# A shared first relu, a moved copy and a swapped sum at the start of a gated-attention kernel

The change halves the first score group's relu between ScalarE and VectorE, lets VectorE rather than ScalarE copy the first turned block of z, and forms the sum of the second output half of the first slot before that of the first.

## Chip, cores and metric

The kernel runs on one core of one Trainium2 chip. The metric is the device time of one execution in microseconds (us). The first three runs of the kernel before gave a median of 1193.32 us (1192.68 to 1193.82). The span of a trace is about 1.8 us shorter than the time of the same run. Kernels are compared only within the same rounds.

## The reference, cut to what matters

```python
# B, S, D = 8, 3008, 256; d_qk = 64; d_ff = 2048
scores = (1.0 / S) * z @ z.transpose(0, 2, 1)
attn = np.maximum(scores, 0.0) ** 2
x = (u * (attn @ v)).reshape(B * S, D)
h = x @ w_in
out = ((h * np.cos(h)) @ w_out).astype(np.float32)      # 24064 x 256
```

The scores are symmetric, so the kernel computes a block (J, I) once and gets (I, J) by transposing it.

## The kernel before

Work goes in slots, one for each batch and 512 rows. Each score group is two matmuls into a two-bank accumulator pair E (512 columns each); ScalarE takes the relu into r (fp16); VectorE squares r into a piece A; and value matmuls multiply A by v into the accumulators M[0], M[1] or into a pair E. `gate_sum` adds two accumulators into an SBUF tile `sm`, and `gate_mul` multiplies that by the turned u.

```python
    def emit_score(later=None):
        b, J, I, h = groups[done_groups[0]]
        ...
        e = E[take_e()]
        for t in range(2):
            ...
            nc.tensor.matmul(e[:, t, 0:Wt], zT[rows, k * P:(k + 1) * P], zT[rows, J * CW:J * CW + Wt], ...)
        r = rpool.tile([P, 2, CW], FP16, name="r")
        nc.scalar.activation(r[:, :, 0:W], e[:, :, 0:W], AF.Relu)
        ...                                   # square(): A = r * r on VectorE

    def gate_sum(s, b0, b1):
        sm = spool.tile([P, CW], FP32, name="sm")
        nc.scalar.copy(sm[:, 0:W], b0[:, 0:W])
        nc.vector.tensor_tensor(sm[:, 0:W], b1[:, 0:W], sm[:, 0:W], ALU.add)
        return sm
```

Three kinds of transfer share the 16 transfer engines in what follows. GpSimd issues the loads (u, v, z, w_in, w_out). SyncE issues the transposes: of u into uT, and of pieces A into their mirrored pieces (a "turned copy" below). SyncE's queue is in order, so a turned copy that is written after a `turn_u` waits until that u has been loaded (in the trace before, u landed at 29.14 us, its transpose was issued at 29.16 and the next turned copy at 31.19). `hold` makes GpSimd wait for a sum before it issues the next load of u:

```python
    def emit_turns(due, more=0):              # turned copies of A
        ...
        nc.sync.dma_start_transpose(d.rearrange("p (n j) -> p n j", j=P), a)

    def hold(src):
        nc.gpsimd.tensor_copy(mark[:, 0:1], src)

    def phase_a_first(s, n, extra={}):        # slots 0, 1 and 2
        ...
        acc = [pair, M] if s == 1 else [M, pair]
        ...
            if dh > 0 and (k % 4 == 3):
                drop_piece((b, J, k // 4))
                if s > 0:
                    emit_turns((0, 0), 1)
                    if k < 4:
                        turn_u(s)
                    elif k < 8:
                        for d in range(2):
                            gate_mul(s - 1, d, late_sums.pop(0))
            for _ in range(at.get(i, 0)):
                emit_score(later=squares if s == 0 and i == lo else None)
        if s == 0:
            turn_u(0)
        late_sums.extend(gate_sum(s, *acc[dh]) for dh in range(2))
        hold(late_sums[0][0:1, 0:1])
        load_u(s + 1)
```

The start and the order of the first slots:

```python
    cast_z(nc.vector, 0)
    cast_z(nc.vector, 1)
    cast_z(nc.vector, 2)
    ...
    turn_on_pe(0)
    copy_turned(0)                            # ScalarE; all others on VectorE
    turn_on_pe(1)
    copy_turned(1)
    emit_score(later=squares)
    emit_score(later=squares)
    turn_on_pe(2)
    ...
    load_u(0)
    nc.gpsimd.dma_start(w_in16, moe_w_in.rearrange("(k p) f -> p k f", p=P))
    phase_a_first(0, 12, {4: lambda: turn_late(4), 8: lambda: turn_late(5)})
    phase_a_first(1, 12)
    nc.gpsimd.dma_start(w_out16, moe_w_out.rearrange("(k p) f -> p k f", p=P))   # first used near 54 us
    for i in range(2):
        emit_h(0, i)()
    phase_a_first(2, 14)
```

Of the kernel before, what the change touches and what calls it, by code (L numbers as in the profile page):

```python
# [9 lines left out]
FP16 = mybir.dt.float16  # L10
# [4 lines left out]
def kernel(  # L15
# [9 lines left out]
    nc = tc.nc  # L25
    AF = mybir.ActivationFunctionType
    ALU = mybir.AluOpType
# [4 lines left out]
    P = 128  # L32
    H = P // 2
    CW = 512
# [12 lines left out]
    def width(J):  # L47
        return CW if J < NC - 1 else WL
# [9 lines left out]
    rpool = pool("r", 3)  # L58
# [17 lines left out]
    turned = [ppool.tile([P, CW], FP16, name=f"turned{i}", tag=f"M{i % 2}") for i in range(3)]  # L76
# [10 lines left out]
    def new_piece(key):  # L87
        pieces[key] = free_pieces.pop(0)
        return piece_bufs[pieces[key]]

    def piece(key):
        return piece_bufs[pieces[key]]

    def drop_piece(key):
        i = pieces.pop(key)
        if pending.get(i):
            pending[i] = "dropped"
        else:
            free_pieces.append(i)
# [3 lines left out]
    def take_e():  # L103
        i = e_order.pop(0)
        e_order.append(i)
        return i
# [59 lines left out]
    def turn_u(s):  # L166
        t = upool.tile([P, 8, P], FP16, name="uT")
        nc.sync.dma_start_transpose(t, u16s.pop(s).rearrange("p j d -> p (j d)"))
        uTs[s] = t
# [17 lines left out]
    turn_slots = {}  # L187
    done_groups = [0]

    def emit_score(later=None):  # L190
        b, J, I, h = groups[done_groups[0]]
        done_groups[0] += 1
        cut = I == J and not (b == 0 and J < 3)
        W = 2 * P if cut and h == 0 else width(J)
        zT = zTs[b]
        e = E[take_e()]
        for t in range(2):
            k = 4 * I + 2 * h + t
            half = t if h == 0 else 1 - t
            rows = slice(half * H, (half + 1) * H)  # L200
            Wt = min(W, (2 * h + t + 1) * P) if cut else W
            nc.tensor.matmul(  # L202
                e[:, t, 0:Wt],
                zT[rows, k * P:(k + 1) * P],
                zT[rows, J * CW:J * CW + Wt],
                start=True,
                stop=True,
            )
        key = (b, J, I)
        a = new_piece(key) if h == 0 else piece(key)  # L210
        r = rpool.tile([P, 2, CW], FP16, name="r")
        nc.scalar.activation(r[:, :, 0:W], e[:, :, 0:W], AF.Relu)  # L212
        def square():
            if I > J:
                a4 = a.rearrange("p (k t j) -> p t k j", k=4, j=P)[:, 2 * h:2 * h + 2, :, :]
                r4 = r.rearrange("p t (k j) -> p t k j", j=P)
                nc.vector.tensor_tensor(a4, r4, r4, ALU.mult)  # L217
            else:
                a4 = a.rearrange("p (k w) -> p k w", w=CW)[:, 2 * h:2 * h + 2, 0:W]
                nc.vector.tensor_tensor(a4, r[:, :, 0:W], r[:, :, 0:W], ALU.mult)  # L220

        if later is None:
            square()
        else:
            later.append(square)
        if h == 0:
            return
        if cut or (I > J and (b, J, I) not in direct):
            turns.append(((b, I), key))
            turns.sort(key=lambda t: t[0])  # L230
            turn_slots[key] = pieces[key]
            pending[pieces[key]] = "held"

    def emit_turns(due, more=0):
        while turns and (turns[0][0] <= due or more > 0):
            if turns[0][0] > due:
                more -= 1
            (b, c), key = turns.pop(0)
            b, J, I = key
            i = turn_slots[key]  # L240
            a = piece_bufs[i]
            if I == J:
                a4 = a.rearrange("p (k w) -> p k w", w=CW)
                for rr in range(1, 4):
                    rows = P if J * 4 + rr < NB - 1 else H
                    nc.sync.dma_start_transpose(
                        a4[:, 0:rr, rr * P:rr * P + rows],
                        a[0:rows, rr * CW:rr * CW + rr * P],
                    )
            else:  # L250
                d = new_piece((b, I, J))
                nc.sync.dma_start_transpose(d.rearrange("p (n j) -> p n j", j=P), a)
            if pending.pop(i) == "dropped":
                free_pieces.append(i)
# [10 lines left out]
    def emit_value(b, J, k, t, dh, bank, start, stop):  # L265
        nc.tensor.matmul(  # L266
            bank[:, 0:width(J)],
            vs[b, k // 4][t * H:(t + 1) * H, k % 4, dh * P:(dh + 1) * P],
            value_rhs(b, J, k, t),
            start=start,  # L270
            stop=stop,
        )

    def gate_sum(s, b0, b1):
        W = width(s % NC)
# [4 lines that stand above are left out]
# [69 lines left out]
    late_sums = []  # L349
    mix_at = {9: ("s2", 0), 19: ("s2", 1), 29: ("s4", 0), 35: ("s4", 1)}  # L350

    def hold(src):
        nc.gpsimd.tensor_copy(mark[:, 0:1], src)

    def phase_a_first(s, n, extra={}):
        b, J = s // NC, s % NC
        ea = e_order.pop(0)
        pair = [E[ea][:, 0, :], E[ea][:, 1, :]]
        acc = [pair, M] if s == 1 else [M, pair]
        last = NB - 1  # L360
        run = 1 if s == 0 else 2
        steps = [
            (dh, k)
            for I in range(0, NC, run)
            for dh in range(2)
            for k in range(4 * I, min(4 * (I + run), last))
        ] + [(2, last)]
        lo, hi = 5 if s == 0 else 2, 42
        at = {}
        for i in range(n):  # L370
            p = lo + (hi - lo) * i // (n - 1)
            at[p] = at.get(p, 0) + 1
        for i, (dh, k) in enumerate(steps):
            if i in extra:
                extra[i]()
            if dh == 2:
                emit_value(b, J, last, 0, 0, acc[0][0], False, True)
                emit_value(b, J, last, 1, 1, acc[1][1], False, True)
            else:
                for t in range(2):  # L380
                    emit_value(
                        b, J, k, t, dh, acc[dh][t], k == 0, k == last - 1 and t != dh
# [11 lines that stand above are left out]
                emit_score(later=squares if s == 0 and i == lo else None)  # L394
        if s == 0:
            turn_u(0)
        late_sums.extend(gate_sum(s, *acc[dh]) for dh in range(2))
        hold(late_sums[0][0:1, 0:1])
        load_u(s + 1)
        e_order.append(ea)  # L400
# [251 lines left out]
    def cast_z(eng, g):  # L652
        dst = z16s[0][:, 4 * g:4 * g + 4, :].rearrange("p k (t d) -> p k t d", t=2)
        eng.tensor_copy(dst, z32[g].unsqueeze(2).to_broadcast([P, 4, 2, dqk]))

    def turn_on_pe(g):
        for k in range(4):
            nc.tensor.matmul(
                turned[g][:, k * P:(k + 1) * P], z16s[0][:, 4 * g + k, :], id16,
                is_transpose=True, start=(k == 0 and g < 5), stop=(k == 3),  # L660
            )

    def copy_turned(g):
        dst = zTs[0][:, g * CW:(g + 1) * CW]
        if g == 0:
            nc.scalar.copy(dst, turned[g])
        else:
            nc.vector.tensor_copy(dst, turned[g])

    wc = cpool.tile([P, 2, CW], FP16, name="c")  # L670
    nc.scalar.activation(wc[:, 0, 0:P], warm[:, 0:P], AF.Sin)
# [1 line left out]
        nc.tensor.matmul(E[i % 2][:, 0, :], warm[:, 0:P], warm, start=True, stop=True)  # L673
    cast_z(nc.vector, 0)
    cast_z(nc.vector, 1)
    cast_z(nc.vector, 2)
    for g in range(3, NC):
        cast_z(nc.gpsimd, g)
        if g == 3:
# [1 line left out]
    squares = []  # L681
    turn_on_pe(0)
    copy_turned(0)
    turn_on_pe(1)
    copy_turned(1)
    emit_score(later=squares)
    emit_score(later=squares)
    turn_on_pe(2)
    copy_turned(2)
    squares.pop(0)()  # L690
    squares.pop(0)()
    M = [ppool.tile([P, CW], FP32, name=f"M{i}", tag=f"M{i}") for i in range(2)]

    def filler(n):
        for i in range(n):
            nc.tensor.matmul(M[1], warm[:, 0:P], warm, start=True, stop=True)  # L696

    turn_on_pe(3)
    copy_turned(3)
    filler(2)  # L700
    emit_score()
    filler(1)
    emit_score()
# [32 lines left out]
    for s in range(3, NSLOT + 1):  # L736
        b, J = s // NC, s % NC
# [52 lines left out]
```

## Time and profile before

| | value |
|---|---|
| median of the first 3 runs | 1193.32 us |
| span of the trace | 1191.2 us |
| TensorE busy | 1183.7 us, 99% |
| TensorE's wait for the first turned block | 0.25 us at 5.46 us |
| TensorE's wait for the second sum of slot 0 | 0.66 us at 25.07 us |
| output weights (w_out): load issued, landed | 39.09, 53.46 us |
| TensorE reaches the first output matmul, which needs w_out (start of its weight load) | 54.40 us |

A line of a timeline reads: start, length, engine, line of the program, operation, destination <- source, shapes, count, and in brackets how long the engine was idle before and what ended it. The lines themselves are shown in the prediction.

### The profile page before, as it was taken

The numbers are of one execution on the slowest core, as the hardware profiler recorded it, in microseconds if no ns is written. First come the engines' busy times: TensorE is split into PE (matmuls) and PEld (weight loads), VectorE is DVE, ScalarE is ACT, GpSimd is POOL, SyncE is SP. The second block draws the span as 40 slices with busy tenths as digits, with TensorE's granted clock in tenths as the row PEclk, the third lists the DMA queues.
The fourth block names the chain that finished last, engine by engine and source line by source line (L and its number), as shares of the span: only waits on it lengthen the run. The fifth ranks groups of instructions, "written<-read, shape, count | busy, mean of one in ns | idle before, by whom it ended". The sixth has DMA issues, their size and how long they took to land.

```text
span 1191.2 us, 29044 instructions
## 1 busy us (share of the span) xinstructions
PE 1183.7 (99%) x11887; PEld 726.8 (61%) x11887; DVE 1011.5 (85%) x1302; ACT 794.9 (67%) x927; POOL 679.0 (57%) x717
## 2 busy tenths in 40 slices
PE   9999999999999999999999999999999999999998
PEld 4556665665566656666566665656666566665566
DVE  6888888889988898888988889888888888888776
ACT  7966676667666676667676676666766666666454
POOL 3286745657466573755647556476555655545452
PEclk9999999999999999999999999999999999999999
DMA  9999999569995799955999469984798837974301
GB/s 160 175 172 158 115 171 130 102 122 104 173 127 101 123 137 166 126 89 103 155 152 130 86 106 158 168 123 70 120 162 152 122 72 120 173 122 84 65 20 54
DMA packets 449142, 148.00 MB, mean 124 GB/s; under 512 B 401264, under 2 KB 432496, under 8 KB 449008
## 3 DMA queue, kind: packets, MB, share of 16 engines
q1 hardware_dynamic: 368464, 112.93, 56.6%
q0 software_dynamic: 80032, 32.78, 27.7%
q8 instruction: 93, 1.52, 0.5%
q10 hardware_dynamic: 512, 0.43, 0.1%
q14 instruction: 41, 0.34, 0.1%
HBM read 66.32 MB, written 24.64 MB: 76 GB/s over the span
## 4 chain that ended last, share of the span: by engine, by line
PE 98%; ACT 1%; DVE 1%; issue 0%; POOL 0%; DVEq 0%; ACTq 0%
PE E L412 27%; PE M L490 23%; PE M L266 20%; PE E L266 19%; PE E L202 6%; PE M L533 1%; ACT r L212 1%; PE M L468 1%; DVE g L423 0%; PE E L673 0%; DVE sm L278 0%; PE E L533 0%; POOL s L441 0%; PE M L696 0%; ACT c L420 0%
## 5 line engine op out<-in xcount | busy, mean ns | idle before, releaser
L420 ACT ACTIVATE c<-E 128x1024 f16<-128x1024 f32 (+1 forms) x384 | 385.7, 1007 | 216.4 <-PE E L412 214.1
L423 DVE SCALAR_TENSOR_TENSOR g<-E,c 128x1024 f16<-128x1024 f32 (+1 forms) x384 | 458.9, 1197 | 62.0 <-ACT c L420 60.9
L212 ACT ACTIVATE r<-E 128x512 f16<-128x512 f32 (+1 forms) x342 | 328.0, 967 | 112.3 <-PE E L202 106.6
L266 PEld LDWEIGHTS <-v 64*128 64x128 f16 x4512 | 245.7, 94 | 229.6 <-issue 18.8
L412 PE MATMUL E<-x,w_in 128*128 128x512 f16 (+1 forms) x1408 | 354.0, 375 | 0.0
L441 POOL TENSOR_TENSOR s<-g 128x512 f16<-128x512 f16 (+1 forms) x184 | 207.8, 1130 | 189.3 <-DVE g L423 139.4
L266 PE MATMUL M<-A,v 64*128 64x512 f16 (+1 forms) x2256 | 283.0, 372 | 0.0
L266 PE MATMUL E<-A,v 64*128 64x512 f16 (+1 forms) x2256 | 278.0, 371 | 0.0
L442 POOL TENSOR_TENSOR g<-g 128x512 f16<-128x512 f16 (+1 forms) x184 | 219.0, 1190 | 14.4
L412 PEld LDWEIGHTS <-w_in 128*128 128x128 f16 x1536 | 133.1, 98 | 108.9 <-issue 19.5
L490 PEld LDWEIGHTS <-g 128*128 128x128 f16 x2816 | 172.5, 98 | 40.8
L217 DVE TENSOR_TENSOR A<-r 128x1024 f16<-128x1024 f16 x240 | 173.2, 734 | 15.1 <-ACT r L212 14.3
L294 POOL TENSOR_TENSOR x<-sm,uT 128x512 f16<-128x512 f32 (+1 forms) x43 | 48.6, 1131 | 223.5 <-DVE sm L278 223.5
L490 PEld LDWEIGHTS <-s 128*128 128x128 f16 x2112 | 129.4, 98 | 32.1 <-DVE s L448 0.5
L202 PE MATMUL E<-zT 64*128 64x512 f16 (+4 forms) x684 | 128.0, 356 | 1.6 <-DVE sm L278 0.7
L448 DVE TENSOR_TENSOR s<-s,g 128x1024 f16<-128x1024 f16 (+1 forms) x92 | 99.7, 1085 | 2.1 <-POOL s L441 2.1
L490 PE MATMUL M<-w_mix,s 128*128 128x128 f16 x1408 | 94.0, 219 | 0.3 <-POOL s L441 0.3
L490 PE MATMUL M<-w_mix,g 128*128 128x128 f16 x1408 | 93.6, 219 | 0.0
L490 PE MATMUL M<-w_out,g 128*128 128x128 f16 x1408 | 93.6, 219 | 0.0
L220 DVE TENSOR_TENSOR A<-r 128x512 f16<-128x512 f16 (+1 forms) x102 | 80.1, 785 | 8.6 <-ACT r L212 7.6
L202 PEld LDWEIGHTS <-zT 64*128 64x128 f16 x684 | 38.7, 94 | 38.4 <-issue 3.8
L450 DVE TENSOR_TENSOR s<-g,s 128x1024 f16<-128x1024 f16 (+1 forms) x92 | 60.6, 661 | 0.0
(58 smaller groups left out, 636.3 us busy)
## 6 DMA issues: line engine op xcount, KB each, us to landing
out_dram<-o SPq DMA_DIRECT2D x87, 256.0 KB, 2.1
v<-in_v_dram POOLq DMA_DIRECT2D x40, 256.0 KB, 11.5
u<-in_u_dram POOLq DMA_DIRECT2D x40, 256.0 KB, 4.5
A<-A SPq DMA_TRANSPOSE x252, 5.3
z<-in_z_dram POOLq DMA_DIRECT2D x14, 192.0 KB, 10.9
z<-in_z_dram POOLq DMA_DIRECT2D x14, 176.0 KB, 6.8
v<-in_v_dram POOLq DMA_DIRECT2D x8, 192.0 KB, 16.1
u<-in_u_dram POOLq DMA_DIRECT2D x8, 192.0 KB, 3.7
```

The source lines that it names most:

```text
L202: nc.tensor.matmul(e[:, t, 0:Wt], zT[rows, k * P:(k + 1) * P], zT[rows, J * CW:J * CW + Wt], start=True, stop=True,)
L212: nc.scalar.activation(r[:, :, 0:W], e[:, :, 0:W], AF.Relu)
L217: nc.vector.tensor_tensor(a4, r4, r4, ALU.mult)
L220: nc.vector.tensor_tensor(a4, r[:, :, 0:W], r[:, :, 0:W], ALU.mult)
L266: nc.tensor.matmul(bank[:, 0:width(J)], vs[b, k // 4][t * H:(t + 1) * H, k % 4, dh * P:(dh + 1) * P], value_rhs(b, J, k, t), start=start, ...
L412: nc.tensor.matmul(e[:, f, 0:W], w_in16[:, k, ft * P:(ft + 1) * P], x[:, k, 0:W], start=(k == 0), stop=(k == 1),)
L420: nc.scalar.activation(c[:, :, 0:W], e[:, :, 0:W], AF.Sin, bias=half_pi, scale=inv_s2)
L423: return lambda: nc.vector.scalar_tensor_tensor(gs[m][:, 2 * i:2 * i + 2, 0:W], e[:, :, 0:W], 1.0, c[:, :, 0:W], ALU.mult, ALU.mult)
L441: nc.gpsimd.tensor_tensor(s1[:, f, 0:n], g[:, f, low], g[:, lower, low], ALU.add)
L442: nc.gpsimd.tensor_tensor(g[:, f, low], g[:, f, up], g[:, f, low], ALU.subtract)
L448: nc.vector.tensor_tensor(s2[:, f, 0:n], s1[:, f, 0:n], g[:, f, up], ALU.subtract)
L490: nc.tensor.matmul(acc[:, k * P:(k + 1) * P], left[:, ft, k * P:(k + 1) * P], right[:, ft, :], start=(ft == 0 and k == 0), stop=(ft == F - ...
```

## The change

The intent is to fill the start, where ScalarE is the slowest link (a copy of 0.59 us, then two relus of about 1 us one after the other) while VectorE has room; and at the end of slot 0 to free E, which the next score needs at once, before M, which is needed 0.6 us later. The diff, with only context lines cut:

```diff
-    def emit_score(later=None):
+    def emit_score(later=None, shared=False):
 ...
         r = rpool.tile([P, 2, CW], FP16, name="r")
-        nc.scalar.activation(r[:, :, 0:W], e[:, :, 0:W], AF.Relu)
+        if shared:
+            r2 = rpool.tile([P, 2, CW], FP16, name="r")
+            nc.scalar.activation(r[:, 0, :], e[:, 0, :], AF.Relu)
+            nc.vector.tensor_scalar_max(r2[:, 0, :], e[:, 1, :], 0.0)
+        else:
+            nc.scalar.activation(r[:, :, 0:W], e[:, :, 0:W], AF.Relu)
+
         def square():
-            if I > J:
+            if shared:
+                for t, rt in enumerate((r, r2)):
+                    dst = a[:, (2 * h + t) * CW:(2 * h + t + 1) * CW]
+                    nc.vector.tensor_tensor(dst, rt[:, 0, :], rt[:, 0, :], ALU.mult)
+            elif I > J:
 ...
-        late_sums.extend(gate_sum(s, *acc[dh]) for dh in range(2))
+        sums = {dh: gate_sum(s, *acc[dh]) for dh in ((1, 0) if s == 0 else (0, 1))}
+        late_sums.extend(sums[dh] for dh in range(2))
         hold(late_sums[0][0:1, 0:1])
         load_u(s + 1)
 ...
-        if g == 0:
-            nc.scalar.copy(dst, turned[g])
-        else:
-            nc.vector.tensor_copy(dst, turned[g])
+        nc.vector.tensor_copy(dst, turned[g])
 ...
     cast_z(nc.vector, 1)
-    cast_z(nc.vector, 2)
 ...
     copy_turned(0)
+    cast_z(nc.vector, 2)
     turn_on_pe(1)
     copy_turned(1)
+    emit_score(later=squares, shared=True)
     emit_score(later=squares)
-    emit_score(later=squares)
+    squares.pop(0)()
     turn_on_pe(2)
     copy_turned(2)
     squares.pop(0)()
-    squares.pop(0)()
 ...
-    filler(2)
+    filler(1)
     emit_score()
```

## The prediction

> **What bounds the kernel now.** I read the page first, then the waits of TensorE alone, then the timeline and the chain of the first 26 us, where all three edits lie. The page:
>
> ```profile
> span 1191.2 us, 29044 instructions
> PE 1183.7 (99%) x11887; PEld 726.8 (61%) x11887; DVE 1011.5 (85%) x1302; ACT 794.9 (67%) x927; POOL 679.0 (57%) x717
> PE 98%; ACT 1%; DVE 1%; issue 0%; POOL 0%; DVEq 0%; ACTq 0%
> ```
>
> The reader is to see that TensorE is busy 99% of the span and makes up 98% of the chain that ended last. Only the idle time of TensorE (1191.2 - 1183.7 = 7.5 us by busy time) and the slow stretches that its neighbours cause can be won. The waits of TensorE, all of the kernel:
>
> ```profile
> PE E L673 <- DVE s L636: 1.2, 1, 1.2
> PE E L202 <- DVE sm L278: 0.7, 1, 0.7
> PE E L202 <- DVE g L423: 0.4, 1, 0.4
> PE M L490 <- POOL s L441: 0.3, 1, 0.3
> PE E L202 <- ACT zT L666: 0.3, 1, 0.3
> PE E L202 <- DVE zT L668: 0.2, 1, 0.2
> ```
>
> Columns: who waited for whom, us in total, times, longest. Two of these are aimed at: 0.3 for ScalarE's copy of the first turned block, and 0.7 for an accumulator sum at the end of the first slot. The other 4.4 us or so of the 7.5 are outside these waits (start, end, hidden or modelled ends). So whatever happens, the scale is 1 us in 1193. The timeline around the first wait (start, length, engine, instruction, idle before):
>
> ```profile
> 4.15 1.06 PE L658 MATMUL turned<-id,z 128*128 128x128 f16 x8
> 4.82 0.59 ACT L666 COPY zT<-turned 128x512 f16<-128x512 f16 x1 [1.06 <-PE turned L658]
> 5.25 0.42 DVE L668 COPY zT<-turned 128x512 f16<-128x512 f16 x1 [0.67 <-PE turned L658]
> 5.46 1.03 PE L202 MATMUL E<-zT 64*128 64x512 f16 x4 [0.25 <-ACT zT L666]
> 6.11 3.77 ACT L212 ACTIVATE r<-E 128x1024 f16<-128x1024 f32 x4 [0.71 <-PE E L202]
> 7.41 0.39 PE L202 MATMUL E<-zT 64*128 64x512 f16 x2
> 8.75 1.04 PE L266 MATMUL M<-A,v 64*128 64x512 f16 x8
> ```
>
> The same copy costs 0.59 on ScalarE and 0.42 on VectorE. From 6.43 to 11.9 TensorE has no recorded wait: the four filler matmuls are paced by hand so that it doesn't. And around the second wait:
>
> ```profile
> 22.99 0.58 ACT L277 COPY sm<-M 128x512 f32<-128x512 f32 x1
> 23.46 0.60 ACT L277 COPY sm<-E 128x512 f32<-128x512 f32 x1
> 23.74 0.68 DVE L278 TENSOR_TENSOR sm<-M,sm 128x512 f32<-128x512 f32 x1
> 24.34 0.68 DVE L278 TENSOR_TENSOR sm<-E,sm 128x512 f32<-128x512 f32 x1
> 25.07 0.39 PE L202 MATMUL E<-zT 64*128 64x512 f16 x2 [0.66 <-DVE sm L278]
> 25.72 0.61 PE L266 MATMUL M<-A,v 64*128 64x512 f16 x4
> ```
>
> The score at 25.07 writes the accumulator E whose sum comes second; M is written again only at 25.72.
>
> **What the Trainium skill says.** "VectorE: DVE Perf Modes", section "Why PSUM operands drop a tier": a PSUM operand caps VectorE at two elements a cycle, and at one for fp32. The trace agrees: 0.42 us for the fp16 copy of 512 out of PSUM, 0.68 for the sum with an fp32 PSUM operand of 512. The new half relu reads fp32 from PSUM, so I size it at 0.67. "PSUM — Partial Sum Buffer", section "PSUM bank collisions raise a hardware error": ScalarE and VectorE must not be in one bank at once. E is two banks, one for each half, so the two halves could run side by side; no run here shows it yet. "TensorE: Matmul & The Clock Gate", section "What's actually happening": matmuls run at half rate until a free-running window of about 3.4 us was busy. The trace agrees: 512-column matmuls start 0.43 apart up to about 6 us and 0.22 apart after.
>
> **The change part by part.**
>
> *Copy on VectorE, third cast behind it.* The transposes of block 0 end at 4.78. VectorE has finished two casts by 4.24, so its copy starts at 4.81 and ends at 5.23, not 5.41: first scores at 5.27 instead of 5.46, gain 0.19. The moved cast runs 5.14 to 5.57 and the second copy 5.48 to 5.90; the block-2 transposes need the cast only at about 6.24. Free.
>
> *Half relus.* I built the changed program and read what its instructions wait for. VectorE's half waits for a ScalarE count that is reached only when ScalarE's half is done, not for TensorE alone: the tiles r are separate, but the source E is one tile. So I expect the halves in series. The first two scores end at 5.27 + 0.61 = 5.88; ScalarE 5.92 to 6.50 (0.58, as its 512-wide PSUM copies); VectorE 6.53 to 7.20. Before, the whole relu ended at 7.14, having started 0.19 later. So E0 comes free 0.06 later than before, with none of the intended halving. What is gained is ScalarE: its second relu runs 6.42 to 7.44, not 7.03 to 8.05.
>
> *Filler and squares.* Transposes of blocks 2 and 3 at 6.24 to 6.70, one filler, and the third score could start at 6.70 + 0.31 = 7.01 (0.31 is the step from a filler to a score at 7.10 to 7.41). E0 is free at 7.20, so with 0.04 of semaphore it starts at 7.24, against 7.41: ahead by 0.17. Then filler, score, filler, each 0.31 later: fourth score 7.86 (before 8.10, where it waited for the second relu; that now ends at 7.44), first value matmul 8.17 + 0.32 = 8.50 rather than 8.75: ahead by 0.25. VectorE's row behind it: two half squares of about 0.42 (estimate: a 1024-wide one takes 0.69 and starts 0.61 after the one before, a copy of 512 0.42) to 7.86, copy 7.77 to 8.19, the second group's square 8.10 to 8.79. The value matmuls need it at 8.50 + 0.43 = 8.93: slack 0.10. The v tile landed at 8.12: slack 0.38. The rest of VectorE's row reaches the copy of block 4 at 10.67; its next user comes at 10.98.
>
> *Sum order.* E's sum takes M's place: it ends at 24.42 instead of 25.02, and the score at 25.07 starts 0.60 earlier within its stretch. TensorE was done with its earlier matmuls by about 24.25 (24.03 + 0.22), so 0.2 of the wait stays. M's sum then ends where E's did, 25.02, and M's next writer moves from 25.72 to 25.12 on the same clock: slack about 0.06. Gain 0.60.
>
> Sum: 0.25 + 0.60 = 0.85 us, on the path that ends last. From then on TensorE is followed by the other engines; the input tiles of this stage landed 0.6 us or more before TensorE asked for them (v at 13.48 for 14.09, the tightest, output weights 53.46 for 54.40), so an earlier TensorE hits none, though the last is cut to 0.1 if its load does not move too. 1193.32 - 0.85 = 1192.47, say 1192.5.
>
> **The rivals.**
>
> 1. *Halves side by side.* If VectorE's half ran beside ScalarE's, E0 were free at about 6.6 and the third score at 7.01; the lead at the values would be 8.75 - 8.27 = 0.48, in all 1.08: 1192.2. Against it: the wait in the built program.
>
> 2. *VectorE becomes the bound of the start.* It takes over a copy and half a relu, and runs a split square of 2 x 0.42 for 0.69. If the half relu costs 0.2 more than sized, the second square ends after 8.93 and the third score slips too: the lead of 0.25 falls to about nothing and 0.6 remains: 1192.7. For it: 0.10 of slack. Against: the 0.68 row is a close likeness.
>
> 3. *Transfers hold the lead.* The DMA digits are 9 in the first seven slices, so loads could stay at fixed times while TensorE comes sooner, and the load of u behind M's sum is issued 0.35 later on the clock. Then the gain shrinks to 0.3 or so: 1193.0. Against: no wait of TensorE on a transfer in all the kernel, and transposed pieces for slot 3 land 3.7 us or more ahead of use.
>
> 4. *The clock warms later.* Less lead-in gap should not delay it, but the window runs freely; eight transposes and a filler at half rate would cost 0.6 and wipe out the first part. This can fall on either kernel and is noise in both.
>
> **Range and chances.** The three runs before spread 1.1 us (1192.68 to 1193.82), more than the gain, so the noise of a median, about 0.5, sets most of the range and the rivals (1192.2 to 1193.0) the rest: 1191.6 to 1193.4. Two per cent is 24 us; nothing here touches the 1150 us that follow. Faster by over 2%: 0.003; slower: 0.004, for a contention I don't see; within: 0.993.
>
> **What would show it right or wrong.** In the changed profile: TensorE's wait for ScalarE's turned copy gone and replaced by one under 0.1 for VectorE's; VectorE's half relu starting right after ScalarE's half ends (if it starts with it, rival 1); third score at 7.2 to 7.3 and first value at about 8.5; the wait for the sum down from 0.66 to about 0.2; the accumulator M not waited for; the later waits (0.4 on g, 0.3 on POOL) unchanged; matmul time unchanged but for one filler. I am wrong if the first value matmul is no earlier than 8.7, if the wait for the sum stays above 0.4, or if a wait on a transfer appears.

## The result and the profile after

| | before | after |
|---|---|---|
| median of 6 runs | 1194.12 us | 1195.47 us |
| range | 1192.68 to 1197.46 | 1194.69 to 1196.62 |
| span of the trace | 1191.2 | 1194.3 |

The ratio after over before is 1.0008, with a 95% interval of 0.9994 to 1.0023: the same within two per cent, as predicted. But 1195.47 us lies above the range of 1191.6 to 1193.4, and where 0.85 us were to be won, the trace is 3.1 us longer. A ratio here is the mean time of one kernel's fast runs over that of the other's of the same rounds, so it is not quite the ratio of the medians quoted. The runs of the kernel before spread too, which is why the ratio says less than the two traces.

The page of the kernel after:

```profile
span 1194.3 us, 29044 instructions
...
PE 1184.9 (99%) x11886; PEld 727.1 (61%) x11886; DVE 1012.6 (85%) x1305; ACT 793.3 (66%) x926; POOL 678.5 (57%) x717
...
PE 95%; DMA 1%; issue 1%; ACT 1%; DVE 0%; POOL 0%; ACTq 0%; POOLq 0%
```

TensorE has one matmul fewer and yet 1.2 us more busy time, and a share of the chain that ended last now belongs to transfers (DMA 1%); before, none was listed. The waits of TensorE after (who for whom, us in total, times, longest) name the transfer:

```profile
PE M L544 <- DMA w_out<-in_moe_w_out_dram: 2.1, 1, 2.1
PE E L681 <- DVE s L647: 1.2, 1, 1.2
PE E L202 <- DVE zT L676: 0.4, 2, 0.3
PE E L202 <- DVE g L434: 0.4, 1, 0.4
PE E L202 <- DVE r L215: 0.3, 1, 0.3
```

The wait of 0.7 us for the sum has left the list. A wait of 2.1 us for the output weights has come in, and the waits of 1.2, 0.4 for g and, cut here, 0.3 us are as before.

**The start came out at the predicted time.** The timeline after, first group:

```profile
5.40 0.60 PE L202 MATMUL E<-zT 64*128 64x512 f16 x4 [0.26 <-DVE zT L676]
5.83 0.60 ACT L214 ACTIVATE r<-E 128x512 f16<-128x512 f32 x1 [2.09 <-PE E L202]
...
6.46 0.69 DVE L215 TENSOR_SCALAR r<-E 128x512 f16<-128x512 f32 x1 [0.17 <-ACT r L214]
...
7.20 0.39 PE L202 MATMUL E<-zT 64*128 64x512 f16 x2 [0.34 <-DVE r L215]
...
8.49 0.82 PE L276 MATMUL M<-A,v 64*128 64x512 f16 x6
```

VectorE's half starts at 6.46, when ScalarE's half has ended at 6.43: in series, as the built program's waits said. It takes 0.69 us (sized at 0.67), and the first value matmul starts at 8.49 (predicted 8.50; before 8.75). But two misses cancel on the way. The first scores start at 5.40, not 5.27, and TensorE's wait for the first block is 0.26 us, not under 0.1: in this trace the first casts began later (3.79 against 3.48 us), when their z had landed. And ScalarE follows the scores by 0.43 us (5.83), where 0.65 had been counted as before (6.11 after 5.46): the clock granted to TensorE reached full speed at 4.83 us in this trace and at 6.40 in the one before.

**The sum did too.** The timeline after, end of slot 0:

```profile
23.48 0.68 DVE L288 TENSOR_TENSOR sm<-E,sm 128x512 f32<-128x512 f32 x1
24.08 0.68 DVE L288 TENSOR_TENSOR sm<-M,sm 128x512 f32<-128x512 f32 x1
24.22 0.39 PE L202 MATMUL E<-zT 64*128 64x512 f16 x2
...
24.82 0.68 POOL L363 CAST mark<-sm 1x1 f16<-1x1 f32 x1 [11.27 <-DVE sm L288]
```

The score that writes E starts at 24.22 instead of 25.07, after only 0.07 us of wait. TensorE is 0.85 us ahead, and at its wait for g it is still 0.86 ahead (39.02 us against 39.88). But the last line is the seed of the loss. GpSimd's mark, which gates the load of the next u, now reads the sum that ends last: it ran 24.49 to 24.67 before and runs 24.82 to 25.50 now. The load is issued at 25.45 instead of 24.72. That the mark takes 0.68 us rather than 0.18 is part of the delay. During the mark VectorE works on the other sum before (24.34 to 25.02, one operand in PSUM), and on a square after (24.77 to 25.46, both operands in SBUF). So it is in all the traces: the mark of slot 0 takes 0.18 us where it falls beside a sum, and 0.67 or 0.68 where it falls beside a square. That the square holds it up is argued from this, not tested.

**Then it is lost at one point.** The chain that ended last, at the place of the new wait (start, length, what):

```profile
38.23 17.78 DMA w_out<-in_moe_w_out_dram
...
56.06 1.89 PE M L544 x8
```

The output weights' load was issued 0.86 us earlier than before, following TensorE, and landed 2.56 us later (56.02 against 53.46): 17.8 us rather than 14.4. TensorE stood for 2.14 us. What follows the stall is seen in the stretches of two microseconds around it (us from:to, length, then busy us and count of PE, PEld, DVE, ACT and POOL, granted clock, DMA share, GB/s), of the kernel before:

```profile
56.00:58.00 2.00, 2.00 (x15) 1.29 (x14) 1.82 (x3) 1.02 (x1) 1.97 (x3) 1.00 1.10 149
```

and after:

```profile
56.00:58.00 2.00, 1.94 (x9) 1.34 (x10) 0.57 (x1) 0.00 (x0) 0.00 (x0) 0.51 1.25 246
58.00:60.00 2.00, 2.00 (x9) 0.95 (x8) 0.00 (x0) 0.34 (x1) 0.12 (x1) 0.64 1.23 264
```

The granted clock falls to 0.51 and 0.64. At half rate for all of the first stretch and 72% of the second (0.64 = 1 - 0.72/2) that is 3.4 us at half speed, an estimated loss of 1.7 us. (The clock record of the trace has half speed from 56.03 to 59.45 us.) The sum closes: at the wait for GpSimd's first s tile, which both kernels reach at the same point of their work, TensorE stands at 1172.75 us against 1169.65. That is +3.10 = -0.86 (lead) + 2.14 (wait) + about 1.8 (slow clock). And it is all lost here: matched one by one, the matmuls on w_in that start after 57.2 us before (1388 of them) are each 3.10 us later after.

So the question for the experiments: why does a load that is issued earlier land later, which part of the change does it, and is it the cause of the times and not just of one trace?

### The profile page after: what moved, and what is told of

It is laid out like the page before. It is cut to its first block, busy times and chain, and to the rows that moved or that the text cites. A ratio compares the mean times of both kernels' runs of the same rounds, so it can differ in the third digit from the quotient of the medians.

```text
span 1194.3 us, 29044 instructions
## 1 busy us (share of the span) xinstructions
PE 1184.9 (99%) x11886; PEld 727.1 (61%) x11886; DVE 1012.6 (85%) x1305; ACT 793.3 (66%) x926; POOL 678.5 (57%) x717
## 4 chain that ended last, share of the span: by engine, by line
PE 95%; DMA 1%; issue 1%; ACT 1%; DVE 0%; POOL 0%; ACTq 0%; POOLq 0%
PE E L423 27%; PE M L501 23%; PE M L276 20%; PE E L276 18%; PE E L202 5%; DMA w_out<-in_moe_w_out_dram 1%; PE M L544 1%; PE M L479 1%; ACT r L217 1%; PE E L681 0%; PE E L544 0%; DVE g L434 0%; DVE sm L288 0%; POOL s L452 0%; POOL u L148 0%
## 5 line engine op out<-in xcount | busy, mean ns | idle before, releaser
L217 ACT ACTIVATE r<-E 128x1024 f16<-128x1024 f32 x341 | 326.9, 966 | 111.6 <-PE E L202 106.0
L453 POOL TENSOR_TENSOR g<-g 128x512 f16<-128x512 f16 (+1 forms) x184 | 218.7, 1189 | 14.4
L227 DVE TENSOR_TENSOR A<-r 128x1024 f16<-128x1024 f16 x240 | 172.9, 732 | 14.4 <-ACT r L217 13.7
L230 DVE TENSOR_TENSOR A<-r 128x1024 f16<-128x1024 f16 (+1 forms) x101 | 79.8, 790 | 8.5 <-ACT r L217 7.9
```

The costliest lines, as they stand in the source:

```text
L227: nc.vector.tensor_tensor(a4, r4, r4, ALU.mult)
L230: nc.vector.tensor_tensor(a4, r[:, :, 0:W], r[:, :, 0:W], ALU.mult)
L453: nc.gpsimd.tensor_tensor(g[:, f, low], g[:, f, up], g[:, f, low], ALU.subtract)
```

## The experiments

The theory at the outset: the change wins its 0.85 us and loses more at the output weights, because with the moved u load other transfers fall onto theirs. The rivals: that before and after differ by the spread of the runs alone; that the lead by itself is enough to hit the load; that VectorE's added work does harm later on. Theories formed on the way are told where they arise. All kernels gave correct results. Each had 5 rounds (six own runs in e13 to e15), beside runs of the kernel before in the same rounds.

| run | own runs, median (range) us | ratio to before [95%] | weights' load issued, landed (took), us | TensorE's wait there, us |
|---|---|---|---|---|
| e1_before_again | 1192.77 (1192.70 to 1193.18) | 0.9994 [0.9980, 1.0008] | 38.87, 52.65 (13.8) | none |
| e2_after_again | 1195.64 (1193.89 to 1197.13) | 1.0018 [1.0005, 1.0030] | 38.41, 54.22 (15.8) | 0.16, then 0.99 for a sum |
| e3_before_early_weights | 1192.95 (1192.81 to 1193.60) | 0.9996 [0.9983, 1.0008] | 25.07, 38.57 (13.5) | none |
| e4_after_early_weights | 1192.45 (1191.93 to 1193.13) | 0.9991 [0.9978, 1.0003] | 25.80, 39.36 (13.6) | none |
| e5_sum_order_only | 1195.35 (1194.65 to 1197.17) | 1.0013 [1.0001, 1.0026] | 38.70, 56.38 (17.7) | 2.04 |
| e6_start_only | 1193.11 (1192.91 to 1193.56) | 0.9993 [0.9979, 1.0006] | 38.99, 52.49 (13.5) | none |
| e7_u_load_on_first_sum | 1193.83 (1192.17 to 1194.73) | 0.9997 [0.9984, 1.0010] | 38.37, 52.45 (14.1) | none |
| e8_halves_side_by_side | 1192.42 (1191.73 to 1194.10) | 0.9988 [0.9975, 1.0000] | 25.52, 38.26 (12.7) | none |
| e9_before_late_u | 1193.10 (1192.80 to 1197.24) | 1.0007 [0.9995, 1.0020] | 39.19, 53.35 (14.2) | none |
| e10_uT_behind_two_A | 1192.91 (1192.65 to 1194.49) | 1.0004 [0.9990, 1.0017] | 38.16, 54.29 (16.1) | 0.48 |
| e11_all_three | 1192.06 (1191.88 to 1192.45) | 0.9992 [0.9979, 1.0004] | 24.91, 36.26 (11.4) | none |
| e12_both_u_edits | 1193.34 (1192.65 to 1195.01) | 1.0000 [0.9987, 1.0014] | 38.61, 54.56 (16.0) | 0.40 |
| e13_turned_copy_after_weights | 1196.78 (1194.34 to 1197.87) | 1.0017 [0.9998, 1.0037] | 38.59, 56.94 (18.4) | 2.71 |
| e14_before_later_u | 1196.60 (1195.23 to 1200.20) | 1.0023 [1.0001, 1.0046] | 38.96, 55.12 (16.2) | 0.60, then 1.95 for a sum |
| e15_u_loaded_at_start | 1193.03 (1192.47 to 1194.56) | 0.9989 [0.9970, 1.0007] | 38.11, 53.80 (15.7) | 0.09 |
| e16_turned_copy_behind_u | 1193.38 (1192.49 to 1193.57) | 0.9999 [0.9986, 1.0013] | 38.71, 51.99 (13.3) | none |
| e17_sum_order_early_weights | 1192.53 (1192.27 to 1194.64) | 0.9998 [0.9985, 1.0010] | 26.56, 39.6 (13.0) | none |

The medians of the kernel before in these rounds were 1193.07 (e1 to e4), 1193.80 (e5 to e8), 1193.06 (e9 to e11), 1193.59 (e12), 1193.31 (e13 to e15) and 1193.04 (e16 and e17).

### Is it the output weights' load? e1 to e4

e1 and e2 are the two kernels again with an unused line taken out; they fix the spread and the repeat of the traces:

```diff
-    parts0 = [(4 * g, 4 * g + 4) for g in range(NC)]
```

> The kernel before, with one unused line taken out, to see how its own runs spread and what its trace shows at the load of the output weights. Theory A (the change itself makes that load land later against its use: it moves TensorE ahead by 0.86 us and the load does not follow): this one's trace shows no wait of TensorE on the load, its five runs lie at 1192.5 to 1194, mean clock 1.000, and its fast runs beat the changed kernel's by about 1 to 2 us. Theory B (the load's landing is chance, with either kernel): this one's runs spread from 1192.5 to 1197 like the changed kernel's, some with a mean clock of 0.998 or 0.999, and the two means lie within 0.8 us of each other.

> The changed kernel, with the same unused line taken out. Both theories: the first 40 us as in its first trace (first value matmul at 8.49, second wait for g at 40.15). Theory A: TensorE waits for the output weights in this trace too, 1 to 3 us, and the times lie at 1194.5 to 1196.5. Theory B: the wait comes and goes, times from 1192 to 1197, the ones without it at 1192.4.

e3 and e4 are the same two kernels with the load of the output weights one slot earlier, so that it cannot be late:

```diff
+    nc.gpsimd.dma_start(w_out16, moe_w_out.rearrange("(k p) f -> p k f", p=P))
     phase_a_first(1, 12)
-    nc.gpsimd.dma_start(w_out16, moe_w_out.rearrange("(k p) f -> p k f", p=P))
```

> Kernel before, with the load of the output weights issued after the first slot (about 25 us) instead of after the second (39 us). If the load's landing is what costs runs their extra microseconds, TensorE has no wait on it, the clock is 1.000 in every run, and times close up to 1192.5 to 1193.3, the fastest of the kernel before. If the spread has another cause, it stays. It may delay the turned copies of u and A on the same DMA engines: a new wait at slot 1 or 2 would show that.

> The changed kernel with the same earlier load. If the prediction's 0.25 + 0.60 is right and only the load took it back, this is 0.8 to 0.9 us faster than the kernel before with the earlier load (about 1191.7 to 1192.4), with no wait of TensorE on a transfer. If the lead is lost elsewhere as well, it is within 0.3 us of it.

Measured: the loss comes back in e2 (mean 1195.69 us, against 1192.88 in e1), and all of it goes with the load in e4 (1192.46 against 1193.04 in e3). e4 has no wait on a transfer, its wait for g comes 0.84 us ahead of e3's (38.81 against 39.65), and its span is 0.9 us shorter (1190.1 against 1191.0). So the predicted gain was there, 0.84 us in the steps of these two traces and 0.6 us in the means, and the late weights hid it. Spread alone falls as an explanation of the loss: e2's interval, 1.0005 to 1.0030, leaves out 1.

e2 shows that the same lateness can take another way. There the weights land at 54.22 and cost only 0.16 us, but a turned copy that was issued at 38.35 us beside them came late too, at 53.61. VectorE, in order, stood at a square that needed its buffer, so the sum behind the square was late, and the output matmul that follows waited 0.99 us for that sum:

```profile
53.70 1.29 DVE L227 TENSOR_TENSOR A<-r 128x1024 f16<-128x1024 f16 x2 [2.35 <-DMA A<-A]
...
55.65 0.81 PE L544 MATMUL M<-w_out,g 128*128 128x256 f16 x6 [0.99 <-DVE sm L288]
```

### Which part of the change? e5 and e6

e5 is the kernel before with the sum order alone; e6 is the kernel after with the sum order undone:

```diff
 # e5, in the kernel before (e6 takes the same two lines back in the kernel after)
-        late_sums.extend(gate_sum(s, *acc[dh]) for dh in range(2))
+        sums = {dh: gate_sum(s, *acc[dh]) for dh in ((1, 0) if s == 0 else (0, 1))}
+        late_sums.extend(sums[dh] for dh in range(2))
```

> Kernel before with the sum order alone (E's sum first in the first slot), nothing else. By the prediction's working the wait of 0.66 us for the sum falls to about 0.1 and the second wait for g moves from about 40.8 to 40.2. Theory A (any lead eats the margin of the output-weight load, which was 0.9 to 1.5 us in the two traces of before): a lead of 0.6 leaves some margin, so runs are mixed, from 1192.2 to 1196, mean near the kernel before. Theory C (the later load of u, which waits for M's sum and so is 0.5 to 0.7 us later here, is what pushes the weights' landing back): stalls as often as in the changed kernel, times of 1194 to 1197.

> The changed kernel with the old sum order: the start's part alone (copy on VectorE, third cast moved, first relu in two halves, one filler less). First value matmul at about 8.5, wait for the sum still 0.66, second wait for g about 0.25 earlier than before. Theory A: a lead of 0.25 hardly touches the margin: times as the kernel before, mostly 1192.5 to 1193.2 with some stalled runs. Theory C: no later load of u here, so as the kernel before too. If it is stalled as often as the changed kernel (1194 to 1197), neither holds, and it is the start's reordering that matters.

Measured: e5 has the whole loss (1195.35 us, the load 17.7 us long, a wait of 2.04), though its wait for the sum is down to 0.06 us. e6 has none (1193.11 us, load 13.5 us long), and its wait for the sum is 0.66 us as before. VectorE's added work at the start is cleared; the sum order carries the loss (in the same rounds, 1.0001 to 1.0026 for e5 and 0.9979 to 1.0006 for e6).

### The lead, or the later u load? e7, e9, e10 and e12

The sum order does two things: TensorE leads by 0.6 us, and the next u is loaded later. e7 keeps the change and lets `hold` wait for the sum that is formed first; e9 is the kernel before with the later u load and no lead:

```diff
-        hold(late_sums[0][0:1, 0:1])
+        hold(late_sums[1 if s == 0 else 0][0:1, 0:1])
```

> The changed kernel, but the load of the next u waits for the sum that now comes first (E's), so that it is issued 0.6 us earlier, at about 24.3. Theory C: the output weights land before TensorE wants them again, times 1191.8 to 1193. Theory A: it stays stalled, 1194 to 1197.

> Kernel before with one edit: the load of the next u after the first slot waits for the sum that comes second (E's, 25.02) instead of the first (24.43). Every engine's order is the same; TensorE gains no lead. Theory C (the later u load pushes the output weights back): the load of u is issued at 25.2 or later, the weights land at 54.2 or later, TensorE waits for them up to 2 us, and the runs lie at 1194 to 1198. Theory A (only the lead matters): as the kernel before, mostly 1192.6 to 1193.2.

Measured: in e7 the u load is back at 24.50 us, the weights take 14.1 us, nothing waits, and the traced run is 1192.17 us. But three of its five runs are at 1193.8 or more, so the remedy holds in some executions only. In e9 the u load is at 25.71, later than after's, and yet the weights take 14.2 us; one of its five runs is long (1197.24). A u load later by a microsecond, without a lead, does not suffice as a rule.

e10 keeps the change, and puts the transpose of the late u behind more turned copies, so that they need not wait for it. e12 does both that and e7's edit:

```diff
-                    if k < 4:
+                    if k // 4 == (2 if s == 1 else 0):
                         turn_u(s)
-                    elif k < 8:
+                    if k // 4 == 1:
```

> The changed kernel with the turned copy of that u moved behind two turned copies of A in the transfer queue that issues them in order. If theory C works by the queue standing still while it waits for u (nothing of it moved from 28 to 29.5 in the stalled traces), the A copies start at about 27.5, more of them are done by 38, the weights land at 53 or before, and the runs come to 1192 to 1193.2. If it stays at 1194 to 1197 the queue's standing still is not the way it works.

> The changed kernel with both edits on the u path: its load on the first sum (e7) and its turned copy behind two copies of A (e10); the output weights load where they did. Theory D, from the nine traces so far (it is the time between the issue of that u load and the issue of the output weights, in which the turned copies of A run: 14.4 us where the weights land 13.5 to 14.4 us after issue, 12.8 where they take 15.8 to 17.8): the gap here is 13.8 or more and the A copies also start sooner, so the weights land in under 14.2 us and before TensorE wants them, and all five runs lie at 1191.9 to 1193.0. If runs at 1193.7 or above stay, as with e7 and e10 alone, chance in the transfers is left even so.

Measured: both are between the extremes (16.1 and 16.0 us of load, waits of 0.48 and 0.40 us, some long runs). In e12 there are 13.9 us between the issue of the u load (24.74) and that of the weights (38.61), against 12.8 in after, and the weights are still late; e7, with the same 13.9 us, had them in 14.1. So the theory that this interval decides by itself fell.

### The lead and its remedies: e8, e11 and e17

e8 has the weights early and gives the second half of the first group a PSUM tile of its own, so that the two relu halves have no common source (cut here: the PSUM tags of the first turned blocks and the target of the fillers, which make room for it):

```diff
+    half_e = ppool.tile([P, CW], FP32, name="half_e", tag="M0")
 ...
-                e[:, t, 0:Wt],
+                half_e[:, 0:Wt] if shared and t == 1 else e[:, t, 0:Wt],
 ...
-            nc.vector.tensor_scalar_max(r2[:, 0, :], e[:, 1, :], 0.0)
+            nc.vector.tensor_scalar_max(r2[:, 0, :], half_e, 0.0)
```

> The changed kernel with the earlier load of the output weights, and the second half of the first score group written to a PSUM tile of its own, so that VectorE's half waits for TensorE only. If one shared source tile was what put the halves in series, VectorE's half now starts at its own copy's end (about 6.2 to 6.3) instead of after ScalarE's half, the wait of about 0.4 before the third score goes, the third score starts at about 6.8 and the first value matmul at 8.1 or a little later (VectorE's squares may hold it), 0.3 to 0.4 us ahead of the changed kernel, and the whole 0.3 ahead of e4: about 1192.1, span 1189.8.

Its timeline:

```profile
5.58 0.60 ACT L216 ACTIVATE r<-E 128x512 f16<-128x512 f32 x1 [1.82 <-PE half_e L204]
5.68 0.68 DVE L217 TENSOR_SCALAR r<-half_e 128x512 f16<-128x512 f32 x1
```

Now the halves overlap, the third score starts at 6.72 us (7.20 after, 6.90 in e4, whose start is the closer match), and TensorE's wait for g comes 0.27 us ahead of e4's. This is what the change meant to do and did not. The medians of e4 and e8 (1192.45 and 1192.42) do not tell the two apart.

e11 is e8 with e7's `hold`:

> The version that the runs point to: the changed kernel with the earlier load of the output weights, halves side by side, and the u load on the first sum. Best so far is e4 and e8 at 1192.4. Same lead as e8 (second wait for g at 39.7), no wait on a transfer; 1191.7 to 1192.5, every run below 1193.5 if the late u load was what made one run of e8 1194.1.

It has the lowest median of all, 1192.06 us, its five runs lie within 0.57 us, and it has no wait on a transfer. Against the kernel before in its rounds (median 1193.06) the ratio's interval, 0.9979 to 1.0004, still holds 1, so it is probably faster by a microsecond, and not shown to be. It is the version I would keep.

e17 is e5 with the weights early:

> Kernel before with the sum order alone and the output weights loaded early. e5 without the early load was at 1195.35, e3 (early load alone) at 1192.95. If the sum order itself is worth its 0.6 us and only the weights took it back: 1192.2 to 1192.6, every run below 1193.5, no wait on a transfer. If it is at 1194 or more, the sum order costs something else.

It goes from e5's 1195.35 to 1192.53 us (one run of five at 1194.64), without a transfer wait. Some 0.8 us of this lies between the rounds, whose medians of the kernel before were 1193.80 and 1193.04; against those, the intervals are 1.0001 to 1.0026 and 0.9985 to 1.0010. The sum order by itself does no harm that these runs show when the weights cannot be late. Its start was slow (the first value matmul at about 9 us, for a late clock), so its wait for g, at 39.56, shows little of the 0.6 us.

### What makes the load slow? e13 to e16

Counting what the transfers moved from 38 to 52 us divides the traces. Where the weights landed early it was 2.35 to 2.50 MB (before, e1, e6, e7, e9), where they were late 2.00 to 2.17 MB (after, e2, e5, e10, e12, e13, e14, e15). So the engines moved less as a whole; it is not that something else took more. GpSimd's issue of the load is not it either: it takes 1.18 us before and 1.17 after. By queue (packets, MB, share of the 16 engines' time; q0 carries GpSimd's loads, q1 SyncE's transposes), the kernel before:

```profile
q0 software_dynamic: 1992, 1.21, 75.8%
q1 hardware_dynamic: 4438, 1.12, 52.9%
```

and the kernel after:

```profile
q0 software_dynamic: 1832, 1.13, 70.9%
q1 hardware_dynamic: 3695, 0.93, 59.2%
```

and e6, where the load was quick (13.5 us):

```profile
q1 hardware_dynamic: 4629, 1.17, 51.3%
```

After, the transposes' packets are fewer but take a larger share of the time. By these lines (share x 16 engines x 14 us, over the packets) one takes about 27 ns before, 25 in e6 and 36 after. This divides all traces with the load at its old place: 25 to 27 ns where the weights landed early (before, e1, e6, e7, e9), 34 to 38 where they were late, 31 in e16 below. Turned copies are beside the load in both. Counted from the one at 21.6 us, the fourth is still under way when the load is issued (it lands at 42.14 us before, 40.17 after), and the fifth starts at 39.03 us before (landing at 48.19) and at 37.78 after (landing at 50.49). The sixth follows at once, and then a transpose of u. The theory formed here: the weights' load is slow for as long as it shares the engines with turned copies, and the later u load, which holds the in-order queue, pushes more of them onto it. Its second half does not fit the counts: while the load was quick, the transposes moved 1.12 to 1.19 MB in these 14 us, and 0.84 to 1.01 MB while it was slow. The Trainium skill, "DMA: Bandwidth & Descriptors", section "Queues, rings and completion order", says that each of the 16 engines goes round-robin between the queues that have work for it, one packet at a time. I had not read that page for the prediction. It makes sharing plausible; what the sharing costs it does not say.

e13 tries to keep the fifth turned copy from starting beside the load, by emitting it later in the program:

```diff
-                    emit_turns((0, 0), 1)
+                    if s > 1 or k < 19:
+                        emit_turns((0, 0), 1)
```

> The changed kernel with the fifth turned copy of A (issued at 37.8 to 43.5, beside the load of the output weights) moved from the first slot's successor into the slot after it. Theory E (the weights land late because they share the transfer engines with turned copies of A): from 40 to 43 us the weights' load has the engines nearly alone, they land at 52 or before, TensorE waits for nothing there, runs at 1191.9 to 1193.0. The copies that it delays are wanted after 72 us and landed 3.7 us ahead in the first trace; a new wait near 74 would show if that is too tight. If the weights still take 15.8 us or more, sharing with that copy is not it.

Measured: 1196.78 us, the longest load of all (18.4 us). The edit missed its aim: SyncE has nothing to wait for at that place, so the copy was issued at 38.40 us all the same. The run tells nothing against the theory, and nothing for it.

e14 makes the u load later still in the kernel before, with no lead: `hold` on the second sum, and a memset on GpSimd ahead of the load:

```diff
-        hold(late_sums[0][0:1, 0:1])
+        hold(late_sums[1 if s == 0 else 0][0:1, 0:1])
+        if s == 0:
+            nc.gpsimd.memset(s4[:, 0:4, :], 0.0)
```

> The kernel before with its next u load about 1.5 to 2 us later (second sum, and a fill of an idle tile on GpSimd in front), so that the chain of turned copies behind it is later by that, and no lead. Theory E: the fourth turned copy of A is issued less than 2.9 us ahead of the weights, which then take 15.8 us or more; TensorE waits for them 0.5 us or more, and most runs lie at 1194 to 1197. If only the lead counts: as the kernel before.

Measured: 1196.60 us, all six runs at 1195.23 or more. The u load goes out at 26.38, the fifth and sixth turned copies run from 39.27 to 55.23 with the load, and TensorE waits twice, for the weights and for a sum behind a delayed turned copy as in e2:

```profile
PE M L535 <- DVE sm L278: 2.0, 1, 2.0
...
PE M L535 <- DMA w_out<-in_moe_w_out_dram: 0.6, 1, 0.6
```

So the lead is not needed for the loss; a later u load alone is enough, if it is 1.7 us later rather than e9's 1.0 (here with a memset more on GpSimd).

e15 takes the u load out of the chain: u of slot 1 is loaded at the start.

```diff
     load_u(0)
+    load_u(1)
 ...
-        load_u(s + 1)
+        if s > 0:
+            load_u(s + 1)
```

> The changed kernel with the second u loaded at the start, in front of the first weights, so that the queue of turned copies does not stand still at 28 us. Theory E: its turned copy goes out by 25 to 27, the fourth turned copy of A 1 us or more earlier than in the changed kernel, the output weights land before they are wanted, runs at 1191.9 to 1193.0. The cost could be that w_in lands about 2 us later (wanted 10.7 us later than it landed: harmless).

Measured: 1193.03 us, and TensorE waits only 0.09 us for the weights, though their load takes 15.7 us. In the traces so far the weights had landed early where the fourth turned copy was issued 3.1 us or more ahead of them (3.39 before, 2.75 after). Here it is 4.8 us ahead and they are still late, so that rule fell. And a late u load is not needed for a slow load of the weights. A new wait of 1.24 us at 97 us, for an output tile, takes part of the gain.

e16 is a closer test: e13's edit, and in slot 2 the transpose of u is put ahead of that turned copy. This u is loaded just ahead of the weights and is there at 43.9 us, so the in-order queue now holds the copy back by itself.

```diff
                 if s > 0:
-                    emit_turns((0, 0), 1)
-                    if k < 4:
+                    if s == 2 and k < 4:
+                        turn_u(s)
+                    if s > 1 or k < 19:
+                        emit_turns((0, 0), 1)
+                    if k < 4 and s == 1:
                         turn_u(s)
 ...
```

> The changed kernel with the fifth turned copy of A behind the turned copy of the third u in the queue, so that it cannot start before that u has landed at about 43 us. Theory E (sharing with turned copies of A makes the weights late): the weights land 13.5 us or less after issue, at 52 or before, TensorE does not wait for them, and the runs lie at 1191.9 to 1193.2, unless the turned copies that this delays are then late themselves (a wait near 74 us). If the weights still take 15.8 us or more with nothing beside them to 43, sharing with that copy is not the cause.

By queue, from 38 to 52 us:

```profile
q0 software_dynamic: 2208, 1.31, 72.6%
q1 hardware_dynamic: 3481, 0.87, 47.9%
```

Measured: the fifth turned copy starts at 45.22 us instead of 37.78, and the loads get 1.31 MB through instead of 1.13 in the same 14 us. The weights take 13.3 us, shorter than in any other trace with the load at its old place, and land 2.03 us before their use, although the load of u for slot 1 is later still than in after (25.92 us). Nothing waits there, and none of the five runs is above 1193.57. Part of the lead goes in a new wait of 0.64 us at 96.87 us, for VectorE's output tile. So what runs beside the load matters: holding the fifth turned copy back for the first six and a half microseconds of the load, with the load at its old place and the u for slot 1 late, takes the lateness away. But how many turned copies run beside it does not decide it. The load was not alone in e16: the fourth turned copy landed only at 43.49 us. And e6 has the fifth copy issued 0.45 us ahead of the load, just as after has (38.54 and 38.99 us against 37.78 and 38.23), and its load took 13.5 us against 17.8. That sharing is the whole mechanism is therefore not shown, and why the transposes' packets take a third longer in the slow traces stays open.

### All runs together

The kernels with the new sum order and no working remedy (after, e2, e5, e13), and e14, have 28 runs, and none of them is under 1193.89 us. The five kernels with the weights early have 25 runs, and two of them are over 1194.05. The kernel before is in between: 16 of its 56 runs in these rounds are at 1194.05 or more. Each run also has a mean granted clock. All 16 runs, of any kernel, with a mean of 0.998 or less are at 1196.12 us or more, and four of them are runs of the kernel before (1196.83 to 1199.15). That fits a stall with a slow clock after it, as in after's trace. No long run of the kernel before fell on a trace, so for those it is argued, not shown.

## Why the prediction was wrong

1. **The start.** Right in what follows what: halves in series, half relu 0.69 us (0.67). That the first value matmul came at 8.49 (8.50) is luck, since the late block and the early clock cancelled. The runs also show the noise, as rival 4 had it. The granted clock reached full speed at 4.80 us in e1 and at 7.17 in e17, and the first value matmul falls between 8.53 and 9.04 us in the seven traces with the old start, and between 8.08 and 8.72 in the ten with the new one (e8 and e11, with halves side by side, left out). Their means, 8.73 and 8.48, are 0.25 apart, so the size was right on average, and worth less than its two digits in any one pair.
2. **The sum order.** Right, and a little low: the wait fell to 0.07, not 0.2. From the first value matmul to the wait for g it is 31.13 us before and 30.53 after, a gain of 0.60 in this pair. The lead of 0.86 at that point is the predicted 0.85.
3. **The step that failed** is the sentence after the sum: the input tiles land 0.6 us or more early, "so an earlier TensorE hits none, though the last is cut to 0.1 if its load does not move too". It took the landing of the output weights as either fixed or moving along with their issue. The issue did move, by 0.86 us, and the landing moved the other way, by 2.56. The wait on a transfer that the prediction had named as a sign of being wrong appeared, 2.14 us long. The load's duration is not a constant: at its old place it is 13.3 to 14.4 us in six traces and 15.7 to 18.4 in eight, where the transposes beside it moved no more, but their packets took a third longer.
4. **Rival 3 had the right place and the wrong size.** It named the transfers, and even the later u load (0.35 us sized, 0.73 measured, since the mark too takes 0.68 instead of 0.18 us). It counted this as a smaller gain, at worst 1193.0, and spoke against it from the absence of waits before. A slack of 0.94 us on a load of 14.4 is 7% of its duration. It should have asked what else runs in that window and what moves into it.
5. **A stall can cost more than its length.** Neither the prediction nor its rivals had the clock after a stall: 2.14 us of wait brought about 1.8 us more. It need not: after e13's wait of 2.71 us the granted clock was 0.58 and 0.56 in two stretches of 2 us, but after e5's 2.04 and e14's 1.95 it stayed at 1.00.
6. **The range** was too narrow on its upper side. It took its noise from three runs within 1.1 us; nine to eleven runs of the same kernel reach 1199.15.

What stays open: why the transposes, and with them the load, run slower in some traces, and the load 15.7 us in one and 18.4 in another; whether the lead or the late u load matters more (e14 is late without the lead, e15 without the late u); why e7, e10 and e12 are in between and change from run to run, and whether the long runs of the kernel before are the same stall.

## What to carry to other kernels

Before an edit that moves a sum or any other gate, list what waits for that gate, transfers above all, and follow the in-order queue behind it to the next big load: here a reordering that won 0.85 us and moved the gate of a small load by 0.7 us cost 3 us in the trace, thirty microseconds on. Treat a load's time from issue to landing as a quantity that depends on its neighbours, and a slack of less than a tenth of it as no slack. A weight load that is needed once should be issued early where there is room (here one slot earlier), which took this loss and most of the run-to-run spread away.

## What the Trainium skill lacked or had wrong

- "DMA: Bandwidth & Descriptors", on queues and arbitration: the round-robin is told, but not what a load loses beside transposes. Here a load of 1 MB took 13.3 to 14.4 us or 15.7 to 18.4 us, and all queues together moved 2.35 to 2.50 MB (2.21 in e16) or 2.00 to 2.17 MB in the same 14 us, with about 25 to 27 ns for a packet of the transposes (31 in e16) or 34 to 38.
- "TensorE: Matmul & The Clock Gate", section "What's actually happening": it gives an idle window of about 3.4 us as the condition for the slow clock. Here 2.14 us without a matmul were followed by granted clocks of 0.51 and 0.64 in the next two stretches of 2 us, and 2.71 us in e13 by 0.58 and 0.56, while 2.04 us in e5 left the clock at 1.00. The length of the slow stretch, an estimated 3.4 us, agrees with the window that the section gives.
- "PSUM — Partial Sum Buffer", section "PSUM bank collisions raise a hardware error": different banks at the same time are said to be clean, and e8 agrees (ScalarE from 5.58, VectorE from 5.68 us, correct results). What no page told me is that the built program orders two engines that read halves of one PSUM tile, though these are two banks: VectorE's half began 0.03 us after ScalarE's had ended.
